# An attention and gated-product kernel written anew: head pairs, score sessions, casting loads

## The chip, the cores and the metric

The kernel runs on one core of one Trainium2 chip. The metric is the device time of one execution in microseconds (us). The core has a matrix engine (TensorE, PE in the profile), a vector engine (DVE), a scalar engine (ACT), GpSimd (POOL) and SyncE (SP), which here only issues DMAs. Each engine takes its instructions in the order in which the program lists them. Products land in PSUM, eight banks of 128 x 512 float32, and another engine must copy them out before a bank can be used again.

## The reference

Causal attention over 4 batches, 8 heads, 768 positions and a head size of 64, and behind it a product with a gate. Heads 0, 2 and 6 see every earlier position; the other five see the first 4 positions (sinks) and a window of 64.

```python
scores = scale * np.matmul(q, k.transpose(0, 1, 3, 2))
stream_keep = causal & (is_sink | in_win)          # heads 1, 3, 4, 5, 7
a = np.exp(scores) / sum                           # masked, softmax
attn = np.matmul(a, v)                             # (4, 8, 768, 64)
x = attn.transpose(0, 2, 1, 3).reshape(3072, 512)
h = x @ w_in                                       # 512 -> 2048
g = h * (1.0 / (1.0 + np.exp(-beta * h)))
out = g @ w_out                                    # 2048 -> 512, float32
```

## The kernel before, in words

The 3072 rows are cut into eight chunks: half a sequence (384 rows) of one batch each. A chunk goes through these steps, all in bfloat16 with float32 sums:

- Loads. Chunks 0 to 2 load k and q in float32, one pair of heads at a time (`load_pair`, L379, on SP and two on ACT), and DVE or ACT cast them (`qkb`, L280). Chunks 3 to 7 load rows on POOL's queue, which cast on the way (`load_rows`, L417). V always comes in float32 on SP (`load_v`, L392) and is cast by DVE, ACT or POOL. The weights come in four quarters each on POOL (L399, L405); a small copy on POOL (`held`, L368) holds each back until a named earlier load has landed.
- Transposes of k and q: on TensorE for chunks 0 to 2 (L448), by DMA on SP later (L462). For the five window heads the sink keys and values are copied together with those of the window (KO, VO).
- Scores. A pair of heads (p, p + 4) sits in the two 64-row halves of the array. Pair by pair, blocks of 128 x 128 (one key tile by one query tile) are computed (L603), three to a bank, with four of the eight banks (`S_BANKS`); chunks 0 and 1 get their mask added by a matmul ahead (L590), later chunks a product on DVE after the exp (L630, L637, L644, L648). ACT takes the exp of each bank (L615). A first half has 22 blocks on the longer side of its pairs, a second half 42.
- Values: one matmul for each block with 65 columns, the last for the sum (L663); then reciprocal and product on DVE (L667, L671), and the transpose of x on TensorE (L683) or by DMA (L688).
- First product, 16 groups of four matmuls (L701), each followed by tanh on ACT (L703) and a gate on DVE (L705), which uses sigmoid as half of one plus tanh.
- Second product, 3 x 16 matmuls (L719), copied out by ACT or DVE (L730, L732) and stored (L735). It shares the other four banks (`G_BANKS`) with all else.

The order on every engine is set ahead by `Plan.run`: a list of tasks with modelled durations, of which each engine takes the one with the lowest key among those that could start first. On TensorE attention comes first, then the first product, with the second product of a chunk some 16 groups behind it. The order of chunks alternates two batches, so that chunks 0 and 1 are both first halves. Zero matmuls fill TensorE's modelled holes early on (L821).

Of the kernel before, what the change touches and what calls it, by code (L numbers as in the profile page):

```python
# [16 lines left out]
class Slots:  # L17
# [18 lines left out]
    def take(self, n):  # L36
        order = sorted(range(len(self.free)), key=lambda i: (self.free[i], i))[:n]
        for i in order:
            self.free[i] = INF
        return order  # L40


class Hold:


    def __init__(self, slots, n=1):
        self.slots, self.n = slots, n
        slots.holds.append(self)
        self.got = None
        self.users = 0  # L50
        self.until = 0.0

    @property
    def buf(self):
        return self.slots.names[self.got[0]]

    @property
    def bufs(self):
        return [self.slots.names[i] for i in self.got]


class Task:
    __slots__ = ("name", "alts", "deps", "prio", "emit", "take", "drop", "mode", "land", "n_wait", "after",
                 "done", "start", "engine", "bias", "seq", "follow")

    def __init__(self, name, alts, deps, prio, emit, take=(), drop=(), mode=128, land=None, bias=0.0, follow=()):
        self.name, self.alts, self.prio, self.emit = name, alts, prio, emit
        self.deps = [d for d in deps if d is not None]
        self.take, self.drop, self.mode, self.land, self.bias = list(take), list(drop), mode, land, bias
# [5 lines left out]

class Plan:
# [3 lines left out]
    SWITCH = 100.0  # L80

    def __init__(self):
        self.tasks = []
        self.fill = None
# [7 lines left out]
    def run(self, pick):  # L92
        free = dict.fromkeys(self.SEM, 0.0)
        ready = {e: [] for e in self.SEM}
        for t in self.tasks:
# [4 lines left out]
        def enter(t):  # L100
            for e, occ, lat in t.alts:
                at = max((d.start if e == d.engine == "PE" else d.done + self.SEM[e] for d in t.deps), default=0.0)
                at = max([at] + [d.start for d in t.follow])
                ready[e].append((at, t, occ, lat))
        for t in self.tasks:
            if not t.n_wait:
                enter(t)
        self.order = []
        self.mode = 128
        dma_free = 0.0  # L110
        lanes = {"hw": [], "sw": []}
        n = len(self.tasks)
        left = n
        while left:
            best = None
            for e, lst in ready.items():
                first = INF
                floor = free[e]
                cand = []
                for it in lst:  # L120
                    at = max(floor, it[0])
                    need = {}
                    for h in it[1].take:
                        if h.got is None:
                            need[h.slots] = need.get(h.slots, 0) + h.n
                            if not h.slots.turn(h):
                                at = INF
# [56 lines left out]
ROUNDS = 2  # L184
# [680 lines left out]
```

## Time and profile before

| what | value |
|---|---|
| runs | 235.86, 236.01, 238.44 us |
| median | 236.01 us |
| profiled execution, span from first to last instruction | 236.1 us |
| mean granted TensorE clock of that execution | 0.993 |
| HBM read, written | 27.27 MB, 6.29 MB |

No device time is listed apart for the profiled execution; its span stands for it. PE is the matrix engine's matmuls, PEld its weight loads, which overlap them. A matmul's row in a timeline holds its passage through the array too, so the distance between the starts of two matmuls, and not their duration, tells what one costs. An engine's row names in brackets how long it stood idle and what released it.

### The profile page before, as it was taken

To read this page: it belongs to the slowest core of one execution; us is meant where nothing else is said; L and a number is where in the kernel's file an instruction comes from. 1 tells how busy PE (TensorE), PEld (TensorE's weight loads), DVE (VectorE), ACT (ScalarE), POOL (GpSimd) and SP (SyncE) were. 2 spreads that over 40 slices of the span, in tenths; PEclk is the share of its full clock that TensorE was granted. 3 is DMA by queue.
4 is the path that set the end of the run, shared out by engine and by line. 5 is a ranking of instruction groups with operands and counts; after the bars stand their busy time and mean duration, and the time that the engine had idled before them with its cause. 6 is when DMAs were issued, how large, how long until landed. Compare 5 with 4: busy or idle time off the path is not lost.

```text
span 236.1 us, 5174 instructions
## 1 busy us (share of the span) xinstructions
PE 227.0 (96%) x1898; PEld 125.8 (53%) x1898; DVE 147.6 (63%) x350; ACT 157.3 (67%) x339; POOL 75.8 (32%) x152
## 2 busy tenths in 40 slices
PE   7969989989999999999999999999999999999994
PEld 3546565544655545555554554555555555555553
DVE  5874878786857546558983886677756443434320
ACT  2947959797745569749786886889975645555400
POOL 4302431841991781799921334030000000000000
PEclk9997999999999999999999999999999999999999
DMA  6999999999899999999994696472121001111112
GB/s 199 247 212 230 174 172 261 254 176 100 158 168 186 158 199 152 122 193 229 130 174 105 148 131 117 109 149 61 21 78 47 24 22 46 47 44 44 44 47 89
DMA packets 93482, 31.10 MB, mean 132 GB/s; under 512 B 79744, under 2 KB 90512, under 8 KB 93456
## 3 DMA queue, kind: packets, MB, share of 16 engines
q1 hardware_dynamic: 56688, 22.10, 41.3%
q0 software_dynamic: 35904, 8.13, 41.0%
q10 hardware_dynamic: 864, 0.53, 0.7%
q8 instruction: 15, 0.25, 0.5%
q14 instruction: 11, 0.09, 0.1%
HBM read 27.27 MB, written 6.29 MB: 142 GB/s over the span
## 4 chain that ended last, share of the span: by engine, by line
PE 87%; DMA 5%; DVE 3%; SPq 2%; ACT 1%; issue 1%; ACTq 0%
PE bank L719 36%; PE bank L701 35%; PE bank L603 7%; PE bank L663 5%; DMA qs<-in_q_dram 5%; SPq L392 1%; PE bank L448 1%; PE bank L590 1%; PE bank L683 1%; SPq L379 1%; DVE gT L705 1%; DVE x L671 1%; ACT es L615 1%; ACT th L703 0%; DVE qkb L280 0%
## 5 line engine op out<-in xcount | busy, mean ns | idle before, releaser
L703 ACT ACTIVATE th<-bank,beta_h 128x384 f32<-128x384 f32 x128 | 74.4, 585 | 39.6 <-PE bank L701 31.7
L705 DVE SCALAR_TENSOR_TENSOR gT<-th,bank 128x384 bf16<-128x384 f32 x128 | 70.2, 551 | 46.8 <-ACT th L703 42.3
L701 PE MATMUL bank<-xT,w_in_sb 128*128 128x384 bf16 x512 | 95.9, 326 | 0.2 <-ACT xT L280 0.2
L719 PE MATMUL bank<-w_out_sb,gT 128*128 128x512 bf16 (+1 forms) x400 | 96.0, 371 | 0.0
L701 PEld LDWEIGHTS <-w_in_sb 128*128 128x128 bf16 x512 | 48.3, 98 | 37.2 <-issue 1.5
L719 PEld LDWEIGHTS <-gT 128*128 128x128 bf16 x400 | 37.0, 98 | 35.5 <-issue 2.6
L615 ACT ACTIVATE es<-bank 128x384 bf16<-128x384 f32 (+1 forms) x96 | 37.5, 477 | 11.6 <-PE bank L603 11.5
L615 ACT ACTIVATE esL<-bank 128x384 bf16<-128x384 f32 x68 | 28.0, 506 | 1.1 <-PE bank L603 1.0
L280 POOL COPY KO<-KT 128x128 bf16<-128x128 bf16 (+3 forms) x23 | 8.0, 370 | 48.5 <-DVE KO L280 17.8
L603 PE MATMUL bank<-QT,KT 64*128 64x128 bf16 (+2 forms) x258 | 22.9, 252 | 0.3 <-ACT QT L280 0.3
L417 POOL DMA_DIRECT2D qs<-in_q_dram x30 | 22.7, 786 | 0.9 <-issue 0.9
L417 POOL DMA_DIRECT2D ks<-in_k_dram x30 | 22.5, 797 | 0.0
L730 ACT ACTIVATE osb<-bank 128x512 f32<-128x512 f32 (+1 forms) x16 | 8.9, 559 | 13.3 <-DVE osb L732 9.9
L603 PEld LDWEIGHTS <-KT 64*128 64x128 bf16 x258 | 10.5, 95 | 13.3 <-issue 11.6
L671 DVE TENSOR_TENSOR x<-bank,rec 128x384 bf16<-128x384 f32 x32 | 17.3, 550 | 0.4
L630 DVE TENSOR_TENSOR es<-es,M 128x768 bf16<-128x768 bf16 (+1 forms) x24 | 12.5, 529 | 4.9 <-ACT es L615 4.9
L732 DVE TENSOR_SCALAR osb<-bank 128x512 f32<-128x512 f32 (+1 forms) x11 | 6.8, 617 | 10.3 <-PE bank L719 10.3
L667 DVE RECIPROCAL rec<-bank 128x6 f32<-128x6 f32 x32 | 6.0, 191 | 11.3 <-PE bank L663 11.2
L663 PEld LDWEIGHTS <-es 128*128 128x128 bf16 x268 | 10.6, 98 | 3.9 <-issue 0.7
L663 PE MATMUL bank<-VX,es 128*128 128x65 bf16 x200 | 11.6, 195 | 0.2 <-DVE gT L705 0.2
L280 POOL COPY VO<-VX 128x512 bf16<-128x512 bf16 (+2 forms) x7 | 6.0, 860 | 9.1 <-PE bank L603 5.3
L663 PEld LDWEIGHTS <-esL 128*128 128x128 bf16 x204 | 7.0, 97 | 1.1
(76 smaller groups left out, 149.9 us busy)
## 6 DMA issues: line engine op xcount, KB each, us to landing
vs<-in_v_dram SPq DMA_DIRECT2D x24, 256.0 KB, 5.4
out_dram<-osb SPq DMA_DIRECT2D x23, 256.0 KB, 2.2
ks<-in_k_dram SPq DMA_DIRECT2D x12, 192.0 KB, 5.9
w_in_sb<-in_moe_w_in_dram POOLq DMA_DIRECT2D x4, 512.0 KB, 8.0
w_out_sb<-in_moe_w_out_dram POOLq DMA_DIRECT2D x4, 512.0 KB, 9.0
qs<-in_q_dram SPq DMA_DIRECT2D x10, 192.0 KB, 8.6
ks<-in_k_dram POOLq DMA_DIRECT2D x30, 64.0 KB, 5.7
qs<-in_q_dram POOLq DMA_DIRECT2D x30, 64.0 KB, 4.3
```

The costliest lines, as they stand in the source:

```text
L280: (nc.scalar.copy if e == "ACT" else eng[e].tensor_copy)(out=out, in_=in_)
L417: ROW[name, c, t] = [dma(f"row{name}{c}.{t}.{a}", "POOL", 750, 850, list(deps), lambda e, t=t, a=a, r=r, i=i, src=src: e.dma_start(out=hol ...
L603: nc.tensor.matmul(to, kk(), of, start=not by_pe, stop=(r, at + n) == ends[a, r] or not by_pe)
L615: EX[a].append(P.add(f"exp{c}.{p}", [act(w * 128)], [t], prio, lambda _, a=a, place=place, w=w, bank=bank: nc.scalar.activation(out=es.buf ...
L630: masks.append(P.add(f"mask{c}.{p}", [dve(2 * (hi - lo) * 128, 0.53)], [EX[0][r], EX[1][r], t_mask], prio, lambda _, lo=lo, hi=hi: nc.vect ...
L663: nc.tensor.matmul(view()[:, i, a, 0:D + 1], es.buf[:, (base[a] + at) * 128:(base[a] + at + 1) * 128], val(), start=(j == 0), stop=(j == l ...
L671: nc.vector.tensor_mul(xo, view()[:, :, :, 0:D], rec.buf.to_broadcast([128, HT, 2, D]))
L701: nc.tensor.matmul(bank.buf[:, 0:HALF], w_in_sb[:, mo, fi * 128:(fi + 1) * 128], XTH[c].buf[:, mo, :], start=(mo == 0), stop=(mo == MO - 1))
L703: t = P.add(f"th{c}.{fi}", [act(HALF, 97)], [t, t_beta], c * 100, lambda _, fi=fi, bank=bank, th=th: nc.scalar.activation(out=th.buf, in_= ...
L705: GATE[c, fi] = P.add(f"gate{c}.{fi}", [dve(HALF)], [t], c * 100, lambda _, fi=fi, bank=bank, th=th: nc.vector.scalar_tensor_tensor(out=GH ...
L719: nc.tensor.matmul(bank.buf[:, 0:hi - lo], GH[c].buf[:, fi, ns * 128:(ns + 1) * 128], w_out_sb[:, fi, lo:hi], start=(fi == 0), stop=(fi == ...
L730: nc.scalar.activation(out=osb.buf[:, 0:h - l], in_=src, func=ACTF.Copy, scale=0.5)
```

## The change

The kernel is written anew around the same arithmetic.

- Chunks run batch by batch: chunk 1 is the second half of the batch whose first half is chunk 0.
- Batch 0 pairs heads (0,1), (3,2), (4,5), (6,7); the other batches keep (p, p + 4).
- Scores of a chunk are laid out as two side lists, one for each half of the array, head after head. A `session` takes banks of four blocks (512 columns) from both lists: seven, seven and six banks for a second half, six and six for a first half, and four sessions for chunk 1. Chunk 0 still goes pair by pair with mask matmuls (L674); chunk 1 is masked on DVE like the later ones. All eight banks are one pool.
- Loads. Chunk 0's heads 0 to 3 come in float32 on SP and ACT; all other k, q of chunks 0 and 1 come four heads at a time as casting loads on POOL's queue (L490), all V as casting loads straight into place (L497), and rows by chunk from chunk 2 on. The weights' quarters stand at fixed places in that queue; nothing holds them back.
- The transposes of k and q of chunks 0 and 1 go head by head, 64 columns out (L542). x is transposed on TensorE for chunks 0, 1 and 7.
- Order on TensorE: a written list (`P.script`) of first-product groups (F1), second-product groups (F2) and sessions; the planner may take a later entry of another kind when the head of the list would wait over 150 ns. Attention's other tasks come ahead of the list.
- The planner's model of DMA queues is new (`Rings`), with costs by packet size.

```diff
+CHUNKS = [(0, 0), (0, 1), (1, 0), (1, 1), (2, 0), (2, 1), (3, 0), (3, 1)]
+STAGE_0 = [(3, 0, 0), (3, 0, 1), (3, 0, 2), (3, 0, 3), (4, 0, None)]
+SESSIONS = {0: [(3, 3), (3, 3)], 1: [(4, 3), (4, 3), (3, 3)]}
+SESSIONS_1 = [(3, 2), (3, 2), (3, 3), (2, 2)]
+ORDER = ["wi0", "wi1", "k1a", "q1a", "k1b", "q1b", "wi2", "wi3", "v10", "v11", "v12", "wo0", "wo1", "wo2", "wo3",
+         ]
 def XT_PE(c, m):
-    return c < 4 or (c == 7 and m % 2)
+    return c < 2 or c == 7
...
-    chunks = [(b0 + i, h2) for b0 in range(0, B, 2) for h2 in range(2) for i in range(2)]
+    NEAR, FAR = [(0, 1), (3, 2), (4, 5), (6, 7)], [(p, NP + p) for p in range(NP)]
+    chunks = CHUNKS
+    PAIR = {c: NEAR if chunks[c][0] == 0 else FAR for c in range(NC)}
...
-    S_BANKS = Slots(banks[0:4])
-    G_BANKS = Slots(banks[4:8])
+    BANKS = Slots(banks)
...
+    def load_sw(c, h, name, prio):
...
+        to = Hold(qkb)
+        t = dma(f"ld{name}{c}.{h}", "POOL", 750, 768, 32, [], lambda e: e.dma_start(
+            out=to.buf.rearrange("p a t d -> p a (t d)"),
+            in_=rows_of(k if name == "k" else q, c)[h:h + 4].rearrange("a (p t) d -> p a (t d)", t=HT)), take=[to], prio=prio, follow=[t_m1])
...
+                for t in range(HT):
+                    for a, (_, hold, i) in enumerate(src):
+                        nc.tensor.transpose(tp[half(a), t, :], hold.buf[:, i, t], ident)
...
+    def session(c, parts, prio, lane):
...
+        work = [(a, lo, SIDE[c, a][1][lo:lo + n], Hold(BANKS)) for a, lo, n in parts]
...
+            for _, a, h, kk, i, n, place, bank, ends in sorted(todo, key=lambda x: x[:2]):
+                nc.tensor.matmul(bank.buf[:, place * 128:(place + n) * 128], kk[1](), QH[c].buf[half(a), WHERE[c][h][1], i * 128:(i + n) * 128], start=not by_pe, stop=not by_pe or ends)
...
+        t = P.add(f"S{c}.{parts[0][1]}", [("PE", occ, occ + 166)], deps + add, prio, go, take=[w[3] for w in work] + [EH[c]], drop=drops, mode=64, lane=lane)
+        for a, lo, part, bank in work:
+            e0 = SIDE[c, a][0] + lo
+            w = len(part)
+            x = P.add(f"exp{c}.{a}.{lo}", [act(w * 128)], [t], prio, lambda _, e0=e0, w=w, bank=bank: nc.scalar.activation(
+                out=EH[c].buf[:, e0 * 128:(e0 + w) * 128], in_=bank.buf[:, 0:w * 128], func=ACTF.Exp, scale=scale), drop=[bank])
...
+        for i, s in enumerate(ses):
+            got.append(s)
+            for _ in range(2):
+                if f2:
+                    got.append(f2.pop(0))
...
+    for c in range(1, NC):
+        P.script += stage(list(F1[c]), list(F2[c - 1]), SES[c + 1] if c + 1 < NC else [])
+    P.script += F2[NC - 1]
```

Three places show what moved. First POOL's order near the start, where the weights are asked for (KO: sink and window keys; `vs`, `qs`: float32 stage buffers; `qkb`, `VX`: bfloat16 targets). Before:

```order
L280 COPY KO_87<-KT_83 128x128
L368 CAST w_in_sb<-vs_79 1x1
L399 DMA w_in_sb<-in_moe_w_in_dram 128x4x512
L280 COPY KO_87<-KT_83 128x128
L280 COPY KO_88<-KT_84 128x128 x2
L368 CAST w_in_sb<-qs_74 1x1
L399 DMA w_in_sb<-in_moe_w_in_dram 128x4x512
```

Now:

```order
L490 DMA qkb_76<-in_q_dram 128x4x192
L497 DMA VX_97<-in_v_dram 128x8x64 x3
L502 DMA w_in_sb<-in_moe_w_in_dram 128x4x512 x2
L490 DMA qkb_77<-in_k_dram 128x4x192
L490 DMA qkb_78<-in_q_dram 128x4x192
L490 DMA qkb_79<-in_k_dram 128x4x192
L490 DMA qkb_80<-in_q_dram 128x4x192
L502 DMA w_in_sb<-in_moe_w_in_dram 128x4x512 x2
L385 COPY KO_93<-KT_89 128x128 x4
L497 DMA VX_98<-in_v_dram 128x8x64 x3
```

Two quarters of w_in moved ahead of chunk 1's keys and queries, and k, q and V came to this queue; the holding copies are gone.

Second ACT's order in chunk 1's attention (`th` is the tanh of the first product of chunk 0, `es` the exps). Before:

```order
L703 ACTIVATE th_110<-bank_70,beta_h 128x384
L615 ACTIVATE es_99<-bank_63 128x384
L615 ACTIVATE es_99<-bank_64 128x384
L615 ACTIVATE es_99<-bank_65 128x384
L280 COPY QT_90<-bank_68 128x384
L615 ACTIVATE es_99<-bank_66 128x384
L703 ACTIVATE th_111<-bank_69,beta_h 128x384
L615 ACTIVATE es_100<-bank_63 128x384
```

Now, the last ten of sixteen exps in a row and what follows them:

```order
L698 ACTIVATE es_104<-bank_69 128x512
L698 ACTIVATE es_104<-bank_68 128x512
L698 ACTIVATE es_104<-bank_63 128x512
L698 ACTIVATE es_104<-bank_64 128x512
L698 ACTIVATE es_104<-bank_65 128x512
L698 ACTIVATE es_104<-bank_67 128x512
L698 ACTIVATE es_104<-bank_66 128x512
L698 ACTIVATE es_104<-bank_70 128x512
L698 ACTIVATE es_104<-bank_69 128x512
L698 ACTIVATE es_104<-bank_68 128x512
L787 ACTIVATE th_114<-bank_63,beta_h 128x384
L787 ACTIVATE th_115<-bank_64,beta_h 128x384
```

The exps of three sessions stand together, over all eight banks, and the tanh behind them.

Third TensorE where scores meet the products (KT keys, QT queries, gT the gated rows). Before, a score group of one matmul between two product groups:

```order
L701 MATMUL bank_68<-xT_107,w_in_sb 128x384
L603 LDWEIGHTS KT_84
L603 MATMUL bank_64<-QT_90,KT_84 128x384
L719 LDWEIGHTS gT_109
L719 MATMUL bank_69<-w_out_sb,gT_109 128x512
```

Now the first matmuls of a session of eighteen:

```order
L804 MATMUL bank_65<-w_out_sb,gT_111 128x512
L689 LDWEIGHTS KT_89
L689 MATMUL bank_64<-QT_95,KT_89 128x256
L689 LDWEIGHTS KT_89
L689 MATMUL bank_69<-QT_95,KT_89 128x256
L689 LDWEIGHTS KT_89
L689 MATMUL bank_64<-QT_95,KT_89 128x128
L689 LDWEIGHTS KT_89
L689 MATMUL bank_69<-QT_95,KT_89 128x128
```

Groups that stood apart between products moved together. TensorE's order now holds 10 score groups ahead of the first second-product matmul and 15 behind it, where it held 14 and 38.

923 lines of the change are left out of this document (507 added, 416 removed).

## The prediction

> **What bounds the kernel now.** I read the page's busy shares first, then who waited for whom on TensorE, the windows, the chain, and last the timelines of single engines.
>
> From the page, busy time by engine:
>
> ```profile
> PE 227.0 (96%) x1898; PEld 125.8 (53%) x1898; DVE 147.6 (63%) x350; ACT 157.3 (67%) x339; POOL 75.8 (32%) x152
> ```
>
> TensorE (PE) is the bound. Its waits, the two longest, and three windows at the start (columns: busy us and instructions of PE, PEld, DVE, ACT, POOL; granted clock; DMA share; GB/s):
>
> ```profile
> PE bank L590 <- ACT es L615: 2.5, 1, 2.5
> PE bank L821 <- DVE zeros L311: 1.3, 1, 1.3
> ```
>
> ```profile
> 12.00:16.00 4.00, 3.69 (x64) 2.48 (x63) 3.72 (x12) 2.15 (x6) 0.29 (x1) 1.00 1.01 209
> 16.00:20.00 4.00, 1.73 (x20) 1.24 (x19) 0.81 (x4) 1.95 (x5) 0.00 (x0) 0.80 1.12 265
> 20.00:24.00 4.00, 3.98 (x41) 2.59 (x39) 2.65 (x7) 3.27 (x9) 1.83 (x5) 0.78 0.83 173
> ```
>
> The one large hole lies at 16 to 20 us, and the clock is down to 0.80 and 0.78 there. Its cause stands in ACT's timeline: a cast of chunk 1's q, in order ahead of chunk 0's last exps, waits for its load. The later rows are the last chunk 1 cast and one group of four exps (384 columns each):
>
> ```profile
> 14.61 0.51 ACT L280 CAST qkb<-ks 128x384 bf16<-128x384 f32 x1 [0.96 <-DMA ks<-in_k_dram]
> 17.43 0.51 ACT L280 CAST qkb<-qs 128x384 bf16<-128x384 f32 x1 [2.31 <-DMA qs<-in_q_dram]
> ...
> 20.73 0.51 ACT L280 CAST qkb<-qs 128x384 bf16<-128x384 f32 x1 [0.75 <-DMA qs<-in_q_dram]
> ...
> 53.71 1.64 ACT L615 ACTIVATE es<-bank 128x384 bf16<-128x384 f32 x4 [0.50 <-PE bank L603]
> ```
>
> After that TensorE has no hole of note. Its work is priced from the chain (start, us, count): first product, second product, values product, and the end.
>
> ```profile
> 98.07 1.73 PE bank L719 x8
> ...
> 135.88 5.20 PE bank L701 x32
> ...
> 174.50 0.90 PE bank L663 x30
> ...
> 222.49 10.41 PE bank L719 x64
> ```
>
> So a first-product matmul costs 5.20/32 = 0.1625 us, a second-product one 1.73/8 = 0.216, a values one 0.030. The last 64 are 32 wide and 32 half-width ones: (10.41 - 32 x 0.216)/32 = 0.109. The tail behind them is 236.1 - 232.9 = 3.2. TensorE's timeline gives the first matmul of each product, a run of transposes, and one group of 12 score matmuls between second-product groups:
>
> ```profile
> 23.66 0.82 PE L701 MATMUL bank<-xT,w_in_sb 128*128 128x384 bf16 x4
> ...
> 41.46 1.03 PE L719 MATMUL bank<-w_out_sb,gT 128*128 128x512 bf16 x4
> ...
> 48.34 0.68 PE L448 MATMUL bank<-idb,qkb 128*128 128x128 bf16 x9
> ...
> 52.38 1.03 PE L719 MATMUL bank<-w_out_sb,gT 128*128 128x512 bf16 x4
> 53.34 0.23 PE L603 MATMUL bank<-QT,KO 64*128 64x128 bf16 x2
> ...
> 53.63 0.22 PE L603 MATMUL bank<-QT,KT 64*128 64x128 bf16 x2
> 53.78 1.04 PE L719 MATMUL bank<-w_out_sb,gT 128*128 128x512 bf16 x4
> ```
>
> The score pairs start 0.29/5 = 0.058 us apart, so both row halves run side by side at one block per 0.057. Around the group, 53.34 - (52.38 + 4 x 0.216) = 0.10 us is lost ahead and 53.78 - 53.63 - 0.06 = 0.09 behind: 0.2 us for each group, whatever its length. The Trainium skill (TensorEngine Tiling (Array Packing), Key Properties) says that a change of tiling mode drains TensorE; the two gaps agree.
>
> **The sum for before.** I cut at the first second-product matmul, 41.46: by then chunks 0 and 1 have their attention, chunk 0 its first product, and one group of four of chunk 1's. Behind it stand 444 first-product matmuls 72.2, second product 368 x 0.216 + 32 x 0.109 = 83.0, 386 values 11.6, score blocks on the longer side (two chunks of 22, four of 42) 212 x 0.057 = 12.1, 38 score groups 7.6, 54 transposes at 0.056 3.0, tail 3.2: together 192.7. Measured: 236.1 - 41.5 = 194.6. The ledger leaves 1.9 unexplained. That profiled span is within 0.1 of the median of 236.01, so the sum holds for the runs too.
>
> **The change past the cut.** At the same cut the new order has all 64 first-product matmuls of chunk 0 behind it and none of chunk 1's. Left: 448 first-product 72.8, second product 83.0, 354 values 10.6 (chunk 1 is now a second half, so one more long chunk lies ahead of the cut), 3 x 22 + 3 x 42 = 192 blocks 10.9, 15 sessions x 0.2 = 3.0, 12 transposes 0.7, tail 3.2: 184.2. I add 2.0 for holes, as before had 1.9, so 186.2. The bounds of the holes are 0.5 and 8. The low end: a session's banks are always free. The high end: each of 15 sessions waits 0.5 us for banks, since it takes six or seven of eight at once, and the two sessions of chunk 2 stand only four second-product matmuls (0.86 us) apart. ACT frees a bank per exp. Its price comes from the group above, (1.64 - 0.50)/3 = 0.38 us apart, and from these two forms:
>
> ```profile
> L615 ACT ACTIVATE es<-bank 128x384 bf16<-128x384 f32 x76 | 31.7, 496 | 11.6 <-PE bank L603 11.5
> ...
> L615 ACT ACTIVATE es<-bank 128x256 bf16<-128x256 f32 x20 | 7.0, 407 | 0.0
> ```
>
> 128 columns more cost 89 ns, so a 512-column exp takes 0.47, and 7 take 3.3 us. Behind most sessions stand eight second-product matmuls (1.7 us) that need one bank, then first-product groups that take banks as exps free them; that is why I stay near the low end. Fewer exps (132 for 164) save ACT 32 x (0.38 - 3 x 0.089 = 0.11) = 3.5 us, worth nothing, since ACT isn't the bound. The V casts that leave DVE and POOL are worth nothing either, beside a dense TensorE; if they did not go, the same cover would hide them.
>
> **The change ahead of the cut.** Loads first. Three weight quarters land this far apart on POOL's timeline; below it, the queues of 24 to 30 us show that nothing but them moved:
>
> ```profile
> 28.65 0.29 POOL L368 COPY w_out_sb<-w_in_sb 1x1 bf16<-1x1 bf16 x1 [2.45 <-DMA w_in_sb<-in_moe_w_in_dram]
> ...
> 31.32 0.18 POOL L368 COPY w_out_sb<-w_in_sb 1x1 bf16<-1x1 bf16 x1 [1.34 <-DMA w_in_sb<-in_moe_w_in_dram]
> ...
> 33.83 0.41 POOL L368 CAST vs<-w_in_sb 1x1 f32<-1x1 bf16 x3 [1.29 <-DMA w_in_sb<-in_moe_w_in_dram]
> ```
>
> ```profile
> q0 software_dynamic: 1053, 1.05, 112.9%
> ...
> q1 hardware_dynamic: 21, 0.00, 0.6%
> ```
>
> 2.6 us each. The DMA rates of 0 to 6 and of 6 to 12 us, in slices of 0.15 us:
>
> ```profile
> GB/s 0 0 0 0 0 0 0 0 0 0 0 0 31 102 46 0 36 195 312 323 364 374 354 369 364 364 379 374 364 364 379 340 338 313 299 338 333 343 312 333
> ```
>
> ```profile
> GB/s 333 338 328 323 312 302 302 268 282 259 273 287 253 237 224 227 222 224 222 224 222 200 178 108 174 258 244 251 246 217 186 145 176 154 191 232 297 338 358 328
> ```
>
> Flow begins at 2.5 us; k and q (1.57 MB a chunk) run at 355 GB/s, 4.4 us, and V (0.79 MB) at 224, 3.5 us. A casting load of k, q or V was not in before. Its bounds are these times (same packets read) and half of them (half the bytes written); I take the first, as POOL's row loads, which cast, moved 128-byte packets no faster than that: in 51 to 54 us, 16 x 3 us / 3188 = 15 ns a packet.
>
> ```profile
> DMA packets 3188, 0.51 MB, mean 169 GB/s; under 512 B 3188, under 2 KB 3188, under 8 KB 3188
> ## 3 DMA queue, kind: packets, MB, share of 16 engines
> q0 software_dynamic: 2306, 0.29, 149.5%
> ```
>
> In the new order of POOL's queue, with 1 us for landing (an estimate): chunk 0's k, q at 8, its V 11.4, w_in quarters 0 and 1 at 14 and 16.6, chunk 1's k, q 21, quarters 2 and 3 at 23.6 and 26.2, chunk 1's V 29.7, w_out quarters 32.3 to 40.1. POOL's first load stands behind four mask instructions; the four loads on SP and ACT (0.79 MB, 2.2 us) cover that. Ahead of w_out quarters 1 to 3 stand copies of chunk 1's keys, which wait for its transposes at 21 to 24; these quarters flow from 31, so that costs nothing unless the transposes are 5 us late. SP loses its V and later k, q loads and keeps transposes and stores. By the 15 ns a later chunk's 9216 packets take 8.6 us, before transposes and stores, of a stage of some 24: hidden. If they were late, SP's queue would hold the x transposes behind Q transposes that wait for rows.
>
> Chunk 0: the 2.5 us wait goes, because no cast of chunk 1 is left in ACT's queue; next in line is ACT itself, 16 exps of at most 0.38 and copies from about 7.3 to 15. First product from 17 (before: 23.7). Chunk 1: its last keys land at 21, TensorE transposes them by 23, scores start at 23.3. From there ACT sets the pace: 16 exps in a row x 0.47 = 7.5, to 31.3, behind which two tanh wait and who waits for them is TensorE, for banks. V is there at 29.7, so it is covered by a second and a half. Then, on TensorE in order, with the DVE steps between: 75 values 2.3, the fourth session and its exps 2, 28 first-product matmuls 4.6, less what overlaps, 8 us in all: cut at 39, within 36 and 43. Ahead of the cut this does 2 us more attention than before did.
>
> The mask matmuls of chunk 1 (16 of the old 32, 2.3 us at most) go from TensorE to DVE, which has room. The transposes by head: 96 of 64 output columns for 72. Their bounds are 0.028 (two halves side by side, as the score pairs) and 0.15: stream 0.056 after its own weight load of 98 ns,
>
> ```profile
> L448 PEld LDWEIGHTS <-qkb x42: 95/98/152, 5.2 to 22.8; 128*128 128x128 bf16 x42
> ```
>
> I take 0.056, the row of the nearest operation; chunk 1's 48 then cost 2.7 us, between 1.3 and 7.2. The Trainium skill (TensorEngine Tiling (Array Packing), Restrictions and Gotchas) says that column tiling disables fast weight load, which speaks for the high end; by it the sum would be the second rival's. No run here shows such a transpose.
>
> Sum: 39 + 186.2 = 225.2, called 225.
>
> **The rivals.** First, sessions that block, on the other side: if TensorE after each session needs all seven exps (3.3 us) before anything but its eight second-product matmuls (1.7), it loses 1.6 x 15 = 24 us: 249. It decides from 0.75 us a session, where the 11 us gained are used up. For it: all banks are one pool now, and tanh queues behind the exps. Against: the eight matmuls and the values products in between need one bank each. Chance 0.06.
>
> Second, a slow ramp: transposes at 0.15 add 7.2 - 2.7 = 4.5: 230. Or the clock: holes of together 4 to 5 us while ACT does the 16 exps, where before one hole of 2.5 us cost (0.20 + 0.22) x 4 = 1.7 us of clock; twice that is 3.4: 228.5. Chance 0.16 together. The Trainium skill (TensorE: Matmul & The Clock Gate, Part 1) gives the clock gate an idle window of about 3.4 us; by that, holes of a microsecond would cost nothing, but here 2.5 us did, so the row decides.
>
> Third, no gain: cut at 42 and 8 us of holes behind it, 42 + 192.2 = 234. Chance 0.06. Fourth, holes of 0.5 and a cut at 34, as casting loads take half the time and ACT's exps start sooner: 219. Chance 0.04.
>
> **How the numbers follow.** Forecast 225 with 0.68, its own span 36 + 184.7 = 221 to 43 + 186.2 = 229. The range 219 to 231 takes in the fourth and second rivals, and leaves out the first and third (0.12) and some tails. Faster by over 1% (about what a measurement tells from no change) is 0.68 + 0.16 + 0.04 = 0.88; within 1% 0.06; slower 0.06.
>
> **What would show it.** First second-product matmul at 39 (36 to 43), first product from 17; 16 exps of 0.47 in one row ending near 31; score groups with 0.2 us around each, 15 behind the cut; a TensorE without holes over 1 us behind it; 186 us from cut to end. I am wrong if the cut comes after 43, if the windows past it show TensorE under 95%, or if the clock leaves 1.00 there.

## The result and the profile after

| | us, median (range) | runs | ratio to before, 95% |
|---|---|---|---|
| before | 237.21 (235.79 to 240.29) | 20 | |
| after | 235.86 (233.92 to 239.1) | 20 | 0.9945 (0.9919 to 0.997) |

The change saves about half a per cent, 1.3 us, where 11 were forecast. 235.86 lies outside the range of 219 to 231. The profiled execution of the changed kernel took 238.22 us, more than most of its runs; where a time matters below I use the profile of the control e1, the same kernel in an execution of 234.63 us with a span of 232.9. A run's time lies some 1.7 us above its span. Ratios leave out executions more than 1.5% above the fastest of their kernel.

The page of after gives TensorE's busy time, then the chain by engine, then the two DMA queues:

```profile
PE 220.0 (93%) x1894; PEld 125.2 (53%) x1916; DVE 137.9 (58%) x340; ACT 148.2 (63%) x291; POOL 98.3 (42%) x154
...
q0 software_dynamic: 70368, 13.25, 78.0%
q1 hardware_dynamic: 32048, 13.25, 29.2%
...
PE 73%; DMA 13%; DVE 4%; POOL 3%; ACT 3%; SPq 2%; issue 1%; ACTq 0%
```

TensorE is busy for 7 us less (227.0 before), but its share fell from 96 to 93%, and the chain passes through DMA for 13% instead of 5%. TensorE's waits, and the windows behind the first second-product matmul (columns as in the prediction):

```profile
PE bank L784 <- DMA xT<-x: 3.5, 4, 1.6
PE bank L689 <- DMA QT<-qr: 3.5, 1, 3.5
PE bank L689 <- ACT es L698: 1.5, 2, 1.3
```

```profile
60.00:80.00 20.00, 15.72 (x133) 8.76 (x132) 11.76 (x31) 10.35 (x23) 16.52 (x26) 0.93 1.97 174
80.00:100.00 20.00, 19.59 (x203) 11.78 (x205) 13.67 (x40) 15.92 (x33) 9.64 (x14) 0.98 1.66 122
100.00:120.00 20.00, 18.15 (x144) 10.15 (x145) 12.41 (x32) 11.31 (x22) 13.00 (x20) 1.00 1.44 155
120.00:140.00 20.00, 18.59 (x155) 10.32 (x156) 11.18 (x28) 14.21 (x27) 12.72 (x19) 1.00 2.21 161
140.00:160.00 20.00, 19.84 (x184) 11.69 (x186) 14.34 (x33) 14.83 (x29) 3.98 (x8) 1.00 0.38 74
```

From 140 us on TensorE is nearly as dense as before. Between 60 and 140 it waits for transposed Q and transposed x, both made by DMA transposes on SP's queue, and around the longest hole the clock falls. So one queue is to be looked at. SP's timeline in the control, 54 to 74 us:

```profile
56.02 0.36 SPq L821 DMA_DIRECT2D out_dram<-osb  x1
56.49 1.23 SPq L556 DMA_TRANSPOSE KT<-kr  x1
57.81 0.53 SPq L821 DMA_DIRECT2D out_dram<-osb  x1
58.44 1.28 SPq L556 DMA_TRANSPOSE KT<-kr  x1
59.81 1.08 SPq L821 DMA_DIRECT2D out_dram<-osb  x1
61.00 1.26 SPq L556 DMA_TRANSPOSE KT<-kr  x1
62.43 1.70 SPq L556 DMA_TRANSPOSE QT<-qr  x1
64.22 2.52 SPq L770 DMA_TRANSPOSE xT<-x  x2
66.91 3.02 SPq L556 DMA_TRANSPOSE QT<-qr  x2
70.03 2.50 SPq L770 DMA_TRANSPOSE xT<-x  x2
72.63 0.52 SPq L821 DMA_DIRECT2D out_dram<-osb  x1
```

From 56.02 to 73.15 SP issues without a pause: six K and Q transposes of chunk 3, four x transposes of chunk 2, four stores (three of chunk 0), 16 us of issue and waits for lanes in 17. Ahead of it, up to 56, it stands behind the first store of chunk 0. The last Q transpose goes out at 68.7 and chunk 3's first scores wait for it until 73.39.

### The profile page after: what moved, and what is told of

It reads as the page before. It is cut to its first block, busy times and chain, and to the rows that moved or that the text cites. A ratio compares the mean times of both kernels' runs of the same rounds, so it can differ in the third digit from the quotient of the medians.

```text
span 236.5 us, 5106 instructions
## 1 busy us (share of the span) xinstructions
PE 220.0 (93%) x1894; PEld 125.2 (53%) x1916; DVE 137.9 (58%) x340; ACT 148.2 (63%) x291; POOL 98.3 (42%) x154
## 2 busy tenths in 40 slices
DMA packets 103305, 27.35 MB, mean 116 GB/s; under 512 B 94688, under 2 KB 100336, under 8 KB 103280
## 4 chain that ended last, share of the span: by engine, by line
PE 73%; DMA 13%; DVE 4%; POOL 3%; ACT 3%; SPq 2%; issue 1%; ACTq 0%
PE bank L784 33%; PE bank L804 30%; DMA xT<-x 8%; PE bank L742 5%; DMA qkb<-in_k_dram 5%; PE bank L689 4%; ACT es L698 2%; DVE gT L789 2%; POOL VX L497 1%; SPq L556 1%; SPq L770 1%; DVE x L752 1%; PE bank L542 1%; POOL qkb L490 1%; POOL w_in_sb L502 1%
## 5 line engine op out<-in xcount | busy, mean ns | idle before, releaser
L804 PE MATMUL bank<-w_out_sb,gT 128*128 128x512 bf16 (+1 forms) x378 | 88.1, 370 | 1.3 <-issue 0.2
L698 ACT ACTIVATE es<-bank 128x512 bf16<-128x512 f32 (+3 forms) x132 | 61.0, 581 | 20.5 <-PE bank L689 20.5
L519 POOL DMA_DIRECT2D kr<-in_k_dram x36 | 27.2, 796 | 8.4 <-DMA w_out_sb<-in_moe_w_out_dram 4.1
L519 POOL DMA_DIRECT2D qr<-in_q_dram x36 | 26.7, 763 | 5.0 <-DMA w_out_sb<-in_moe_w_out_dram 3.0
L497 POOL DMA_DIRECT2D VX<-in_v_dram x24 | 21.5, 928 | 4.6 <-DMA w_in_sb<-in_moe_w_in_dram 4.4
L742 PEld LDWEIGHTS <-es 128*128 128x128 bf16 x472 | 18.0, 98 | 4.2 <-issue 0.5
L742 PE MATMUL bank<-VX,es 128*128 128x65 bf16 x392 | 18.7, 194 | 0.0
L385 POOL COPY KO<-KT 128x12 bf16<-128x12 bf16 (+3 forms) x30 | 8.2, 317 | 21.3 <-PE bank L689 13.3
L718 DVE TENSOR_TENSOR es<-es,Mc 128x384 bf16<-128x384 bf16 x21 | 7.5, 355 | 9.2 <-ACT es L698 9.2
L689 PE MATMUL bank<-QT,KO 64*128 64x128 bf16 x75 | 10.1, 217 | 0.1
```

Source lines behind the costliest of these rows:

```text
L497: LD["v", c, t] = dma(f"ldv{c}.{t}", "POOL", 1000, 256, 64, list(deps) + [t_ones[id(x)] for x in V_r.names], lambda e: e.dma_start(out=VH[ ...
L519: ROW[name, c, t] = [dma(f"row{name}{c}.{t}.{a}", "POOL", 750, 256, 32, [], lambda e, t=t, a=a, r=r, i=i, src=src: e.dma_start(out=hold.bu ...
L689: nc.tensor.matmul(bank.buf[:, place * 128:(place + n) * 128], kk[1](), QH[c].buf[half(a), WHERE[c][h][1], i * 128:(i + n) * 128], start=n ...
L698: x = P.add(f"exp{c}.{a}.{lo}", [act(w * 128)], [t], prio, lambda _, e0=e0, w=w, bank=bank: nc.scalar.activation(out=EH[c].buf[:, e0 * 128 ...
L742: nc.tensor.matmul(view()[:, i, a, 0:D + 1], EH[c].buf[:, e0 * 128:(e0 + 1) * 128], val(), start=(j == 0), stop=(j == len(mine) - 1))
L804: nc.tensor.matmul(bank.buf[:, 0:hi - lo], GH[c].buf[:, fi, ns * 128:(ns + 1) * 128], w_out_sb[:, fi, lo:hi], start=(fi == 0), stop=(fi == ...
```

## The experiments

Theory 1 says that SP's order and load make the holes, theory 2 that POOL's queue brings the rows late, theory 3 that the DMA engines have too many small packets. Ratios are to the kernel before, with 95% intervals. Each edit lets the planner set a new order, which is why the traces are read beside the times.

### Controls (e1, e16)

No edit.

> The changed kernel as it is, for a profile beside the other runs and an own time. Both theories: 0.99 to 1.0 of the kernel before; first second-product matmul at 41 (39 was forecast), TensorE waiting 7 to 9 us in all for x transposes and Q transposes behind it, the longest hole near 72 us.

> The changed kernel as it is once more, on the chip of the other three, so that they can be held against it there. All theories: 0.99 to 1.0 of the kernel before; holes for QT 2.6 to 3.5 and for xT 1.6 to 2.7 us.

e1: 235.2 us, 0.9926 (0.986 to 0.9992). e16: 236.42, 0.9972 (0.9933 to 1.0011). Holes for QT and xT 2.6 and 2.1 us in e1, 3.0 and 3.9 in e16; first second-product matmul at 40.07 and 40.37. The 4.7 us in e1 are less than the 7 to 9 expected, and xT in e16 is above its 1.6 to 2.7.

### SP's load: x transposes on TensorE (e2)

```
 def XT_PE(c, m):
-    return c < 2 or c == 7
+    return True
```

> All x transposes on TensorE: 60 more transposes, 60 x 0.056 = 3.4 us of its time, and 20 DMA transposes fewer in SP's queue. Theory 1 (SP's queue order makes the holes: chunk 3's K and Q transposes stand behind chunk 0's stores and the x transposes behind Q transposes): the 8 us of waits for xT and QT fall under 3, net 2 to 5 us faster than the control. Theory 2 (the rows come late through POOL's queue and busy DMA engines, whatever SP's order): the wait for xT goes, the hole for QT near 72 us stays within 1 us, net 0 to 1 us faster or slower by up to 2.

233.02 us, 0.9822 (0.9764 to 0.988), 2.2 under the control beside it although TensorE transposes 60 blocks more.

```profile
PE bank L689 <- DMA QT<-qr: 2.0, 2, 1.4
PE bank L689 <- ACT es L698: 1.5, 2, 1.3
...
PE bank L764 <- DVE x L752: 1.0, 1, 1.0
```

The xT waits are gone, and the longest QT hole is 1.4 instead of 2.6 (2.0 in two waits). For theory 1 the gain fits at its low end, and a part remains: chunk 3's K transposes still stand behind chunk 0's stores. But the smaller QT hole is not its proof. Q transposes issued last, first in e1 and then in e2 (count, median us from issue to landing):

```profile
QT<-qr SPq DMA_TRANSPOSE x2, 4.7
```

```profile
QT<-qr SPq DMA_TRANSPOSE x1, 8.1
```

The last one is issued 3.8 us sooner in e2 (64.9 for 68.7) and lands 0.2 us sooner (73.0 for 73.2). The hole shrinks mostly because TensorE, with its own transposes, comes to it 0.9 us later.

### SP's order: stores (e3, e13) and x transposes (e14)

e3, e13 and e14, one line each:

```
-                parts = ((lo, hi, "SP"),) if not last
+                parts = ((lo, hi, "ACT"),) if not last
```

```
-                        out=out[n0:n0 + 128, l:h], in_=osb.buf[:, 0:h - l]), drop=[osb], prio=c * 10 + 15)
+                        out=out[n0:n0 + 128, l:h], in_=osb.buf[:, 0:h - l]), drop=[osb], prio=c * 10 + 15, follow=GK[3, 0] if c == 0 else ())
```

```
-                XTD[c, m] = dma(f"Xx{c}.{m}", "SP", 1250, 256, 27, deps, xt, take=[XTH[c]], drop=[XH[c]], prio=c * 10)
+                XTD[c, m] = dma(f"Xx{c}.{m}", "SP", 1250, 256, 27, deps, xt, take=[XTH[c]], drop=[XH[c]], prio=c * 10, follow=GQ[c + 1, 0])
```

> The output stores are issued on ACT's queue instead of SP's, so no transpose on SP stands behind a store. Theory 1 (SP's order): chunk 3's first K transpose is issued before 56 us instead of 57.6, its last Q transpose before 68 instead of 70, and the 3.5 us hole near 72 shrinks to under 1; 3 to 6 us faster than the control. Theory 2 (late rows): the transposes move by less than 1 us, since their rows land no earlier; within 1 us of the control.

> One edit in SP's order: chunk 0's stores may start only behind chunk 3's three K transposes, which in the control stand between and behind those stores from 56 us on. Theory 1 (SP's order): the K transposes go out at 52 to 57 as their rows land, chunk 3's last Q transpose goes out 2 to 3 us before 69.9, the QT hole near 72 falls from 2.6 to under 1 with the clock's dip behind it; 2 to 4 us faster than the control. Theory 2 (POOL's queue) or 3 (DMA packets): the transposes move forward but their rows and landings do not; within 1 us.

> The other edit in SP's order: a chunk's x transposes may start only behind the next chunk's Q transposes. Theory 1, order alone: the QT hole goes and the xT holes stay at 2.1; 2 to 4 us faster. Theory 1, capacity (SP has 1.25 us of issue for each transpose, and any order makes something late in this stretch): the QT hole goes and the xT holes grow by as much; within 1 us of the control. Theory 2 or 3: both holes stay.

e3: 237.78 us, 1.0021 (0.9963 to 1.0079), no gain; theory 1 had 3 to 6. The K transposes do go out sooner, at 53.62, and the QT hole falls to 0.9. But the new order puts two x transposes ahead of the last two Q transposes (63.37 and 66.01), and SP stands idle for x from 61.3 to 63.4. TensorE's and ACT's waits:

```profile
PE bank L784 <- DMA xT<-x: 4.8, 4, 2.1
```

```profile
ACT th L787 <- DMA out_dram<-osb: 8.0, 1, 8.0
```

The second line names a store, now issued on ACT, but it is not what holds the tanh. That tanh reads the first product of chunk 2, whose last matmul starts at 73.83 behind an xT wait; and in the control ACT is idle for 8.47 us at the same place. Most of the loss that shows is the longer waits for xT.

e13: ten runs from 230.85 to 236.34 us, median 234.55 against 236.42 for the control beside it. The ratio, 0.9811 (0.9761 to 0.9861), is formed over five of them. The three quickest, 230.85 to 231.91, are as quick as the version with both edits below. The profiled one (233.2) still has a QT hole of 3.3 us at 74, though K goes out 2.8 us sooner: the last Q transpose, again behind a pair of x transposes, is out only 1.4 us sooner than in e16, and lands no sooner (74.0). So e13 alone settles little. e14: 235.16, 0.9914 (0.9879 to 0.9948). Its waits on TensorE:

```profile
PE bank L784 <- DMA xT<-x: 4.1, 5, 1.2
PE bank L689 <- DMA QT<-qr: 1.8, 1, 1.8
```

The QT hole gives up 1.2 us (3.0 in e16). Chunk 2's x transposes, issued from 67.58 instead of 64.92, are now waited for 2.4 us instead of 0.4. In this stretch that is theory 1 in its form of capacity. The sum is 5.9 us for 6.9, since e16's 1.8 us for chunk 4's x are gone, which this edit does not explain.

### Both together (e15, e17)

The edits of e2 and e13.

> All x transposes on TensorE and chunk 0's stores behind chunk 3's K transposes: SP's queue has nothing left ahead of chunk 3's keys. Theory 1: no QT hole over 0.5 us, clock 1.00 from 60 to 80, 1 to 3 us faster than x transposes on TensorE alone (0.982 of the kernel before, so 0.97 to 0.978). Theory 2 or 3: the QT holes of 2.0 stay, 0.98 to 0.985.

> The kernel of the last call once more (x transposes on TensorE, chunk 0's stores behind chunk 3's K transposes), with more rounds: 0.974 to 0.983 of the kernel before, below 1 by more than its interval; no wait for a transposed tile over 0.5 us behind the first second-product matmul.

231.55 us, 0.9784 (0.974 to 0.9828), and again 231.64, 0.9792 (0.9758 to 0.9825). This version beats the kernel before and the changed one (0.9945). SP's timeline and TensorE's windows in e15:

```profile
53.94 3.89 SPq L556 DMA_TRANSPOSE KT<-kr  x3
57.93 1.54 SPq L821 DMA_DIRECT2D out_dram<-osb  x3
59.64 6.52 SPq L556 DMA_TRANSPOSE QT<-qr  x3
```

```profile
60.00:80.00 20.00, 19.89 (x198) 12.22 (x199) 13.56 (x40) 15.92 (x34) 15.36 (x23) 1.00 1.57 159
80.00:100.00 20.00, 19.70 (x200) 11.86 (x202) 16.41 (x46) 15.65 (x33) 15.91 (x23) 1.00 2.08 160
100.00:120.00 20.00, 19.79 (x161) 11.28 (x161) 12.37 (x34) 13.46 (x28) 17.03 (x23) 1.00 1.74 170
```

No wait for a transposed tile is left, the clock is 1.00 from 36 us on, and the DMA share is as high as ever (1.57 to 2.08 beside 1.92 and 1.66 in the control). Theories 2 and 3 had the QT hole stay. So relieving SP's queue is enough to remove the holes. It does not show that place in the queue was all: the last Q transpose is issued at 65.0, as in e2 (64.9), but lands at 70.5 instead of 73.0, and what sets that time is open. The edits also take 20 transposes off the DMA engines.

### POOL's queue (e4, e7, e5, e6)

e4 makes the V loads of a chunk in the loop behind the next chunk's rows. e7 adds work to POOL:

```
+            for i in range(4):
+                P.add(f"junk{i}", [("POOL", 1, 1)], [F1[0][8 + i]], -500, lambda _: nc.gpsimd.memset(junk, 0.0))
```

> On POOL's queue a later chunk's three V loads stand behind the next chunk's K and Q rows instead of ahead of them. Theory 2 (late rows): chunk 3's rows are issued 2.7 us sooner (three V loads of 0.9), and its Q transposes land 2 to 3 us sooner than 75.4; the hole near 72 shrinks from 3.5 to about 1; 2 to 4 us faster. Theory 1 (SP's order): SP stands behind the first store until 57.2 all the same; the hole stays over 2.5 us, time within 1 us of the control.

> Doubles one suspect: four memsets of 512 columns (about 0.6 us each, 2.4 us together) are put into POOL's queue between chunk 2's row loads, their result unused; nothing else in the program order changes. Theory 2 (POOL's issuing): row loads move back by up to 2.4 us, holes for QT and xT grow by 1 to 2.4 us, 1 to 3 us slower than the control. Theory 1 or 3 (SP's order, DMA packets): POOL has slack behind its lanes; within 0.7 us of the control.

e4: 240.42 us, 1.0111 (1.0032 to 1.019). The QT hole falls to 0.6, but the values now come late: the xT waits grow to 8.8 us (x is made from them), and the clock is 0.84 and 0.83 from 80 to 120 us (the profiled execution took 243.45 us, 2 to 5 more than the others). V cannot give way. For the QT hole, though, theory 2 was right: chunk 3's rows are issued from 43.15 instead of 46.27, its K transposes go out at 49.74, ahead of the first store, and its last Q transpose lands at 67.4 instead of 73.2. Later rows are one reason why these transposes fall behind the stores. e7: 234.69, 0.9881 (0.9805 to 0.9956), not slower than the control: the QT hole is 3.1 for 2.6, xT 2.1 as there. 2.4 us more on POOL cost nothing in the time. But the added work fell into POOL's waits, and from 32 us on the rows are issued 0.3 to 0.4 us sooner than in e1. So POOL's issue has slack there; what later rows would cost e7 does not say.

e5 and e6 bring chunk 2's K and Q by hand, e5 as float32 on SP's queue, e6 by the casting loads:

```
-BY_HAND_C = 2
+BY_HAND_C = 3
...
+                        load_hw(2, h, name, "SP", g, 0, GQ[1, 3])
```

```
-BY_HAND_C = 2
+BY_HAND_C = 3
...
-ORDER = ["wi0", "wi1", "k1a", "q1a", "k1b", "q1b", "wi2", "wi3", "v10", "v11", "v12", "wo0", "wo1", "wo2", "wo3",
+ORDER = ["wi0", "wi1", "k1a", "q1a", "k1b", "q1b", "wi2", "wi3", "v10", "v11", "v12", "wo0", "wo1", "wo2", "wo3", "k2a", "q2a", "k2b", "q2b", "v20", "v21", "v22",
```

> Chunk 2's K and Q come by hand again: float32 loads on SP's queue from about 25 us, casts and 48 transposes of 64 columns on TensorE (about 1.4 to 2.7 us), and POOL's queue carries only its V behind w_out; 12 row loads and 6 DMA transposes go. Theory 2, now sharper (POOL's queue: in the profile of the control chunk 2's row loads wait for lanes behind w_out's quarters, 1.84, 2.31, 1.25 and 1.79 us between 30 and 40 us, so every later row comes about 9 us of issue late): chunk 3's first row is issued near 40 instead of 46.3, the QT hole near 72 and the xT holes fall from 4.7 us to under 2, 2 to 5 us faster than the control. Theory 1 (SP's order): SP's queue still mixes stores, Q and x transposes; the holes stay over 4 us, time within 1 us or, with the transposes, 2 us slower. Theory 3 (the DMA engines' packets are the limit): the float32 loads add traffic beside w_out, w_out lands later than 40, the cut moves from 40 to 42 or more.

> Chunk 2's K and Q come by the casting loads of four heads on POOL's queue, behind w_out: 4 loads instead of 12, 1536 packets of 768 bytes instead of 6144 of 256, and 48 transposes on TensorE. Theory 2 (POOL's queue): chunk 3's rows are issued 4 to 6 us sooner, holes fall by 2 to 4 us, less the transposes 1 to 3 us faster; but chunk 2's keys, behind w_out, may land later than by rows and make a hole before chunk 2's first scores. Theory 1: within 1 us of the control or 2 us slower by the transposes. Theory 3: like theory 2, since the packets fall to a quarter; told apart by the next two.

e5: 239.64 us, 1.0102 (1.0035 to 1.0169). Behind 60 us it is dense, 19.63 of 20 to 80 and 19.84 to 100, but its float32 loads and casts fall into chunk 1's attention: TensorE is busy 5.71 of 8 us from 28 to 36, and the clock is 0.79 there and 0.72 to 42. e6: 232.69, 0.9819 (0.9751 to 0.9887). All waits for QT and xT are gone; 2.2 us are lost between 40 and 60, where scores wait for x (1.3), and the clock is 0.91 behind that. Both free SP of six transposes as well as POOL of row loads, so they do not tell theories 1 and 2 apart, although theory 1, as it was put, had no gain from e6 and the holes of e5 staying.

### DMA packets (e8, e10, e9)

e8 and e10 add 4096 packets of 128 bytes, on ACT's queue and on SP's; e9 takes 16,000 away.

```
+            dma(f"junk{i}", "ACT", 60, 256, 0, [F1[0][8 + i]], lambda e, i=i, junk=junk: e.dma_start(
+                out=junk, in_=v[1, :, i * 128:(i + 1) * 128, 0:D // 2].rearrange("h p d -> p h d")), prio=-0.5)
```

```
+            dma(f"junk{i}", "SP", 1, 256, 0, [], lambda e, i=i, junk=junk: e.dma_start(
+                out=junk, in_=v[1, :, i * 128:(i + 1) * 128, 0:D // 2].rearrange("h p d -> p h d")), prio=c * 10, follow=GQ[2, 0])
```

```
-            out=VH[c].buf[:, t, :, 0:D], in_=rows_of(v, c)[:, t * 128:(t + 1) * 128, :].rearrange("h p d -> p h d")), take=[VH[c]], prio=prio, follow=follow)
+            out=VH[c].buf[:, t, :, 0:D] if c < 2 else VH[c].buf[:, t].rearrange("p h d -> p (h d)"),
+            in_=rows_of(v, c)[:, t * 128:(t + 1) * 128, :].rearrange("h p d -> p h d") if c < 2 else
+            v[chunks[c][0]].rearrange("h s d -> (h s d)")[t * 128 * H * DE:(t + 1) * 128 * H * DE].rearrange("(p x) -> p x", p=128)), take=[VH[c]], prio=prio, follow=follow)
```

> Doubles the other suspect: four loads of 1024 packets of 128 bytes each, on ACT's hardware queue between 33 and 40 us, their result unused, so the DMA engines move 4096 packets more (about 4 us at 15 ns a packet) and POOL and SP issue nothing more. ACT pays 4 issues. Theory 3 (the DMA engines' packets are the limit): rows and transposes land up to 4 us later, holes grow by 2 to 4 us. Theory 2 (POOL's issuing and lanes) or 1: within 1 us of the control.

> The extra traffic once more without ACT: the four loads of 1024 packets of 128 bytes stand on SP's queue between chunk 2's last Q transpose and chunk 0's first store, where SP has nothing to issue for 6 us (50 to 56). Theory 3 (DMA packets): the Q rows and K transposes that move at that time land 2 to 4 us later, the QT hole near 72 grows from 2.6 to 4 or more, 2 to 4 us slower than the control. Theory 2 or 1: within 1 us of it.

> From chunk 2 on, each V load takes 2112 contiguous bytes for a partition instead of eight rows of 256: as many instructions on POOL, 3% more bytes, 128 packets instead of 1024 (18 loads, 16,000 packets fewer). The values read are other ones (and overwrite the columns of ones), so the output differs from the reference; every instruction behind stays. Theory 3 (the DMA engines are short of time for small packets between 40 and 75 us): rows and transposes land up to 896 x 3 x 15 ns x 1/1 / 16 engines' worth, 2.7 us a chunk, sooner; the holes of 4.7 us for QT and xT fall to under 2, 3 to 6 us faster than the control. Theory 2 (POOL's queue): only its lanes come free sooner, 1 to 2 us faster. Theory 1 (SP's order): within 1 us.

e8: 247.11 us, 1.0404 (1.0314 to 1.0494), but for a reason that no theory had. ACT's timeline, the third extra load and the copy behind it:

```profile
46.65 0.39 ACTq L903 DMA_DIRECT2D junk<-in_v_dram  x1
47.13 0.48 ACT L385 COPY xT<-bank 128x384 bf16<-128x384 bf16 x1 [10.44 <-DMA KT<-kr]
```

Loads on ACT's and SP's queues share eight lanes in this program, and this one waited for a K transpose to land; ACT stood 10.4 us and TensorE 9.8. The run says nothing of packets. e10: 236.92, 1.0006 (0.9973 to 1.0039), 0.3 to 0.8% above the controls' ratios. Here too issue comes first: SP spends 7.37 us on the four loads, chunk 3's K transposes go out 2.8 to 3.1 us later, and DVE's copies of these keys make the hole (SP, then DVE, then TensorE):

```profile
49.56 7.37 SPq L864 DMA_DIRECT2D junk<-in_v_dram  x4
```

```profile
70.12 0.57 DVE L385 COPY KO<-KT 128x256 bf16<-128x256 bf16 x2 [4.68 <-DMA KT<-kr]
```

```profile
71.20 4.57 PE L804 MATMUL bank<-w_out_sb,gT 128*128 128x512 bf16 x13 [3.60 <-DVE gT L789]
```

3 us of delay on SP come out as 3.6 us on TensorE, in place of the QT hole of 2.6. That is what theory 1 gives for late K transposes, but the run adds packets as well, so theory 3 is left to e9 (which reads other bytes than V, and so computes another result): 234.34 us, 0.9893 (0.9829 to 0.9957), beside 0.9926 for the control. With 87,177 packets for 103,305 the waits are:

```profile
PE bank L691 <- DMA QT<-qr: 2.9, 1, 2.9
PE bank L786 <- DMA xT<-x: 1.7, 4, 1.0
```

The holes stay, and theory 3's gain of 3 to 6 us does not come. That settles it for the packets of V; those of the K and Q rows and of the transposes are as before.

### Sessions (e11), the two helpful edits together (e12)

```
-SESSIONS = {0: [(3, 3), (3, 3)], 1: [(4, 3), (4, 3), (3, 3)]}
+SESSIONS = {0: [(2, 2), (2, 2), (2, 2)], 1: [(2, 2), (2, 2), (2, 2), (2, 2), (3, 1)]}
```

> Chunks 2 to 7 have their scores in 24 sessions of four banks instead of 15 of six or seven. The step of the forecast on sessions (0.2 us for each change of tiling mode and back, whatever its length): 9 x 0.2 = 1.8 us slower than the control, if nothing else moves. The rival on banks (sessions that take six or seven banks hold TensorE up): the waits for exps, 1.5 us in the control, fall under 0.5, and it is 0 to 1 us faster. Holes for QT and xT stay as they are by either.

> Both edits that helped: chunk 2 by casting loads of four heads, and all x transposes on TensorE. Theory 3: DMA packets fall by 7500 and by 8400 more, no wait on a transposed tile is left, and the 60 transposes cost 3.4 us of TensorE at 0.056 each (1.7 at 0.028): 1 us slower to 2 us faster than chunk 2's casting loads alone, since those already left no wait for xT. Theory 1: the gains add, 4 to 5 us faster than the control.

e11: 237.07 us, 0.9998 (0.9961 to 1.0035), 0.3 to 0.7% above the controls, 0.6 to 1.7 us; but its xT waits are 6.2 us and the QT hole is gone, so its time alone does not price a session (the ledger below does). The waits for exps stayed at 1.5, all before the cut: the rival on banks finds nothing. e12 (edits of e2 and e6): 236.75, 0.9982 (0.9949 to 1.0016). The gains do not add. No transposed tile is waited for, but the new order puts x transposes on TensorE's queue before their x is there, a hole of 2.56 us ahead of 60.87, and the windows from 40 to 80 lose 3.6 us. Neither theory had that time.

### The clock of the ramp (e18)

```
-FILL_END, FILL_SPARE = 16000.0, 120.0
+FILL_END, FILL_SPARE = 40000.0, 120.0
```

on the kernel of e17.

> The same with zero matmuls in TensorE's planned gaps up to 40 us instead of 16 (34 more of 256 columns), for the clock, which falls to 0.79 to 0.82 between 28 and 36 us in some runs. If that dip costs its 0.2 x 4 to 8 us of TensorE's work (0.8 to 1.6 us): clock 1.00 there and the cut at 39.3 or earlier, 1 us faster than without. If ACT's row of exps sets that stretch (the rival): the cut stays at 39.6 to 40.2, whatever the clock, and the time within 0.6 us.

234.31 us, 0.9888 (0.9848 to 0.9928). First 24 to 36 us of e17, then of e18, and the first second-product matmul of each:

```profile
24.00:28.00 4.00, 2.42 (x45) 1.63 (x41) 2.07 (x5) 4.00 (x9) 2.38 (x7) 0.93 1.97 174
28.00:32.00 4.00, 4.00 (x47) 2.59 (x47) 2.86 (x6) 4.00 (x10) 2.17 (x3) 0.64 1.26 207
32.00:36.00 4.00, 3.52 (x65) 2.65 (x61) 3.68 (x11) 3.96 (x10) 1.49 (x2) 1.00 1.24 208
```

```profile
24.00:28.00 4.00, 4.00 (x52) 3.06 (x51) 1.85 (x4) 3.91 (x9) 1.58 (x5) 1.00 1.93 174
28.00:32.00 4.00, 3.96 (x60) 2.95 (x59) 3.15 (x6) 4.00 (x10) 2.59 (x4) 1.00 1.30 204
32.00:36.00 4.00, 3.88 (x65) 3.08 (x64) 3.90 (x11) 3.88 (x10) 0.98 (x2) 1.00 1.25 207
```

```profile
40.13 1.89 PE L804 MATMUL bank<-w_out_sb,gT 128*128 128x512 bf16 x8
```

```profile
40.01 1.89 PE L804 MATMUL bank<-w_out_sb,gT 128*128 128x512 bf16 x8
```

With zero matmuls in the gaps the clock stays at 1.00, and the cut moves by 0.12 us. From the first of the 16 exps to the cut it takes 15.28 us, for 15.33 in e17: ACT, busy 4.00 of 4 us, sets this stretch, and e17's dip is nearly free. That is not so for every dip. Six runs without these matmuls (e2, e6, e7, e9, e10, e14) have the clock at 1.00 here and take 15.17 or 15.18 us; e1, at 0.66 and 0.92, takes 15.91, so its dip cost 0.7 us. From 28 to 36 us, e1 and then e9:

```profile
28.00:36.00 8.00, 7.58 (x98) 5.49 (x93) 6.61 (x17) 7.52 (x17) 3.56 (x6) 0.79 1.26 207
```

```profile
28.00:36.00 8.00, 7.10 (x104) 5.09 (x102) 7.29 (x18) 7.93 (x18) 3.21 (x5) 1.00 1.24 207
```

What e18 loses comes later, in two holes of 1.29 and 0.94 us for masks, from the order that its plan got.

## Why the prediction was wrong, step by step

**The cut at 39.** 40.07 in the control, within the range of 36 to 43. First product from 17: 16.97 after. ACT's 2.5 us wait for a cast is gone. The 16 exps run as one row, 7.95 us (0.50 each; 7.5 was forecast), but from 25.05 instead of 23.8 (24.16 in e1), since chunk 1's scores start at 24.5 for 23.3 (23.62 in e1): chunk 0's first-product groups stand between its transposes. After's timeline:

```profile
16.97 1.30 PE L784 MATMUL bank<-xT,w_in_sb 128*128 128x384 bf16 x7
```

```profile
25.05 7.95 ACT L698 ACTIVATE es<-bank 128x512 bf16<-128x512 f32 x16
```

**The transposes by head.** Runs of 12 take 0.46 to 0.53 us in after's chain, 0.038 to 0.044 each, between the low bound of 0.028 and the 0.056 taken: 48 cost 1.9 us. So that part of the second rival falls.

```profile
19.75 0.53 PE bank L542 x12
...
21.04 0.46 PE bank L542 x12
```

The Trainium skill (TensorEngine Tiling (Array Packing), Restrictions and Gotchas) has column tiling switch off fast weight load, by which the high bound of 0.15 was to be feared; the trace does not show that price here. Its weight loads of 64 columns take 109 ns, where 128 columns took 98 before, but they overlap.

**The clock in the ramp.** The rival said holes while ACT works through its row would cost 3.4 us of clock. They do lower it (0.69 in after, 0.66 in e1, 0.64 in e17). Held against the 15.17 us of the runs at full clock, that cost 1.0 us in after, 0.7 in e1 and 0.2 in e17. So this rival came in part, inside the cut's range. The Trainium skill (TensorE: Matmul & The Clock Gate, Part 1) puts the idle window at about 3.4 us; in after the waits ahead of the dip are 0.22 and 1.25 us, so here shorter waits can be enough. They do not decide it: the same two waits stand in e9, where the clock stayed at 1.00.

**186.2 from the cut to the end: the step that failed.** The control has 192.8, 6.6 more. The text said of the loads "hidden", of SP that it "loses its V and later k, q loads and keeps transposes and stores", and put 2.0 us for holes. It counted the transposes that leave TensorE as a gain (12 left for 54) and not what they issue elsewhere: x of chunks 2 and 3 moves to SP's queue, eight DMA transposes of 1.25 us of issue, chunk 2's K and Q add six, and they meet chunk 0's three stores. The sentence that the x transposes might queue behind Q transposes "if they were late" named the place, and gave it no price. Measured in the control: 2.6 us for QT, 2.1 for xT, and 1.8 of clock (0.91 over the 20 us around the first), 6.5 in all. Two of the prediction's own signs of being wrong show there: TensorE is busy 17.33 of 20 us from 60 to 80, and the clock leaves 1.00.

How much of this is SP's order stays open. The 2.1 us for xT lie at 102 to 104 us (chunk 3) and at 125 (chunk 4, whose x went by DMA before too). For chunk 3, x is ready at 95.55 and its last transpose, issued at 98.2, lands at 104.1; in e13 the same two are issued at 98.5 and 100.1, land 2.3 us later, and TensorE does not wait. From 98 to 104 us POOL's queue moves 4348 packets in e1 and 139 in e13. That points to landing beside POOL's row loads, a part of theory 3 that e9 left as it was; no run tests it.

The 2.0 was something else: e15 has no such hole, and its 189.55 from cut to end stand against 184.2 and 60 x 0.056 = 3.4 for the added transposes, 2.0 short, as the ledger of before was 1.9 short. That remainder seems to lie in the prices of the dense work, which no run takes apart; the holes come on top of it.

**0.2 us a session.** Not measured alone, but three ledgers close with it: with 38 groups before (1.9 over), 15 sessions in e15 (2.0 over), and 24 in e11: 237.0 - 40.1 = 196.9, less 184.2, nine more sessions 1.8, holes 6.2 and 0.7, clock 1.8, leaves 2.2. Without those nine it would be 4.0. Masks of chunk 1 on DVE and V casts off DVE and POOL were not tested alone.

**The base.** The sum was made on spans, 236.1 before, and held against the median of times, 236.01. A time lies 1.7 above its span, and the 20 runs have a median of 237.21. The forecast in the units of the table was 226.9.

Put together for e1: 225.2 + 1.1 (cut) + 6.6 (holes, clock) + 1.7 (base) = 234.6. **The rivals:** the third, no gain, with a cut at 42 and 8 us of holes, comes nearest (40.07, and 6.6 of holes and clock), given 0.06; what held TensorE was not banks but transposed tiles. Sessions that block did not happen; of the slow ramp only the 0.7 us of clock came.

## What to carry to other kernels

An instruction that leaves the bound engine still has to be issued and, as a DMA, to land: count what it puts into each queue, as issue time in that stretch (here 16 of 17 us on SP), not as a share of the stage, and read the time from issue to landing beside it (2.3 to 9.1 us for a transpose in these runs). An in-order queue that carries both what is needed next and what can wait (stores) holds the first behind the second: look at what stands ahead of the next stage's operands. The two edits that cleared it took the time from 0.9945 of the kernel before to 0.979.

## What was not expected of the hardware

- A DMA transpose of a 128x512 or 128x384 tile holds SP for 1.2 to 1.3 us when it goes straight out (1.23 and 1.28 in the control), and the last Q transpose of chunk 3 landed 3.6 (e9) to 8.1 us (e2) after issue.
- 16,000 packets of 256 bytes fewer (e9) brought no transposed tile clearly sooner, though after's page shows the DMA engines at 90% or more in most slices up to 140 us.
- The same two waits of TensorE, 0.22 and 1.25 us, came with a clock of 0.57 to 0.69 in the next 4 us in eleven profiled runs and of 1.00 in six. Those six began chunk 1's scores between 23.76 and 24.12 us, the eleven before or after; whether that is the reason, no run shows.
